# Sliding-window attention and a gated feed-forward block: the first batch loaded by halves of heads, the second transposed 128 wide, and the queues of VectorE and TensorE reordered

## The chip, the cores and the metric

The kernel runs on one core of a Trainium2 chip. The metric is device microseconds of one execution; lower is better. The core has five engines with a queue each, worked off in the order in which the program was recorded: PE (TensorE, matrix products into PSUM), DVE (VectorE), ACT (ScalarE), POOL (GpSimd, which here mostly issues loads) and SP (SyncE, which here issues stores and transposing transfers). "PEld" in the profile is the loading of a product's fixed operand.

## The reference

Eight batches of eight heads, 576 positions, head size 64. A query sees itself and the 127 positions before it, with a penalty that grows linearly with distance and has a slope of its own for each head. The 4608 rows of 512 that result go through a gated feed-forward block with 1536 hidden channels.

```python
B, H, S, D = q.shape                       # 8, 8, 576, 64
scores = np.matmul(q, k.transpose(0, 1, 3, 2)) / np.sqrt(D)
rel = pos[:, None] - pos[None, :]
scores = np.where((rel >= 0) & (rel < 128), scores - slopes * np.abs(rel), -1e9)
attn = softmax(scores)                     # over the keys
x = (attn @ v).transpose(0, 2, 1, 3).reshape(B * S, H * D)
out = (gelu(x @ w_gate) * (x @ w_val)) @ w_out
```

## The kernel before

**Attention.** Inputs are converted to bf16 while they are loaded. The queries and keys of a batch are transposed so that the head size lies on the partitions (`qT`, `kT`); two heads share the 128 partitions, and the four pairs of heads are numbered c = 0 to 3. Positions fall into five blocks of 128 keys, j = 0 to 4, shifted by 64 so that the first half of block 0 is padding. `scores` (L178) makes, for a part s of the queries (part one is queries 0 to 319, part two the rest) and some pairs, the products of keys by queries into PSUM; ACT takes the exponential (L161), and DVE multiplies by a table `emask` that holds penalty and window (L164), in this text "the mask". `scores2` (L166) does the same for block 2 against itself, all pairs in one tile `P2`. `sums` (L203) adds up the probabilities over the keys with products by `ones` and takes the reciprocal on DVE (L218). `spread_pe` (L228) copies the reciprocals to all partitions with products by `sel`, and ACT and DVE bring the result from PSUM into `rb` (L239). `values` (L241) multiplies by v and DVE scales by `rb` into `xT` (L256), the transposed input of the feed-forward block. From batch 4 on the spreading is done by transfers on SP's queue instead.

**Feed-forward.** The 4608 rows are worked in nine groups g of 512. `gate_val` (L262) makes one of 12 hidden channel blocks f of a group: eight products, a gelu on ACT (L273) and a product on DVE (L274). `out_half` (L279) makes half of the sum for 128 output rows, six products; eight such units, numbered 0 to 7, make a group, and after each second one ACT copies the result (L290) and SP stores it. While group g is in work, the attention of a later batch is woven between its units: for g = 0, 1 and 2 the table `todo` writes the order out by hand, from g = 3 on a fixed pattern does it (L399).

**Batches 0 and 1** have to be ready early. Both are loaded in runs (`load_runs`, L101): a partition gets three consecutive positions, or two for the last 192, so that one piece of a transfer holds 192 or 128 numbers; PE transposes them, 64 numbers wide, and the copy out of PSUM puts the positions back into order (`transpose`, `untangle`). Batch 0 does this at the start of the program, batch 1 inside `gate_val` for f = 8 to 11 of group 0, one pair of heads for each f (L412). There both run lengths of a pair go to the same PSUM bank. The batches from 2 on are loaded by blocks of 128 positions (`load`, L81, pieces of 64 numbers) and transposed by transfers on SP's queue.

**What sets the order.** Each engine's queue stands in the order in which the Python code calls it. PSUM has eight banks; `bank()` hands out one that the order has set free, and the product that first writes it waits for the last reader of the tile before. A transfer on POOL's queue waits until the one eight places ahead of it in that queue has landed.

Of the kernel before, what the change touches and what calls it, by code (L numbers as in the profile page):

```python
# [8 lines left out]
BF16 = mybir.dt.bfloat16  # L9
# [17 lines left out]
def kernel(  # L27
# [35 lines left out]
    def bank():  # L63
        return psum.tile([128, 512], FP32, name="ps")
# [23 lines left out]
    def load_qk(b):  # L88
        load(qs[b % 2], q, b)
        load(ks[b % 2], k, b)  # L90
# [4 lines left out]
    def runs(t, n):  # L95
        first, parts, r = RUNS[n]
        lo = 1536 * n
        return t.rearrange("p j x -> p (j x)")[0:parts, lo:lo + 512 * r].rearrange(
            "p (h x) -> p h x", h=H)

    def load_runs(b, n):  # L101
        first, parts, r = RUNS[n]
        for t, src in ((qs[b], q), (ks[b], k)):
            nc.gpsimd.dma_start(
                out=runs(t, n),
                in_=src[b][:, first:first + parts * r, :].rearrange(
                    "h (p r) d -> p h (r d)", r=r))

    def load_v(b):
# [12 lines left out]
    def transpose(b, n, what, c, ps):  # L122

        first, parts, r = RUNS[n]
        src = runs((qs, ks)[what][b], n)
        for x in range(r):
            for i in (0, 1):
                nc.tensor.transpose(  # L128
                    out=ps[64 * i:64 * i + 64, parts * x:parts * x + parts],
                    in_=src[:, 2 * c + i, 64 * x:64 * x + 64],  # L130
                    identity=ident[0:parts, 0:parts])

    def untangle(copy, b, n, what, c, ps):
        first, parts, r = RUNS[n]
        dst = by_pair((qT, kT)[what][b])[:, c, 64 + first:64 + first + parts * r]
        copy(out=dst.rearrange("p (x r) -> p x r", r=r),  # L136
             in_=ps[:, 0:parts * r].rearrange("p (r x) -> p x r", r=r))

    def blocks(t, b, i, c, j, n):
        if b < 2:  # L140
# [34 lines left out]
            exp(P[:, :, i, :], ps[i].rearrange("p (c n) -> p c n", c=4))  # L175
        mask(P.rearrange("p c i n -> p (c i) n"), emask[:, :, 0:128])

    def scores(b, s, cs):  # L178

        pss = []  # L180
        for c in cs:
            ps = [bank(), bank()]
            pss.append(ps)
            for j, qj, n, col in (((0, 0, 2, 0), (1, 1, 2, 256)),
                                  ((4, 4, 1, 0), (2, 3, 1, 128), (3, 3, 2, 256)))[s]:
                for i in (0, 1):
# [110 lines left out]
    for t in qT + kT:  # L297
# [8 lines left out]
    for half, base, step, chan in ((0, 0, 1, -1), (1, -1, -1, 1)):  # L306
# [35 lines left out]
    def rest(cs, copy):  # L342
        for c in cs:
            for w in (0, 1):
                ps = bank().bitcast(BF16)
                transpose(0, 1, w, c, ps)
                untangle(copy, 0, 1, w, c, ps)

    scores(0, 0, (0, 1))
    scores2(0)  # L350
    rest((0, 1), dve)
    scores(0, 0, (2, 3))
    rest((2, 3), dve)
    scores(0, 1, (0, 1))
    sums(0, 0)
    scores(0, 1, (2, 3))
    spread_pe(0, 0)
    values(0, 0, range(4))
# [13 lines left out]
    for t in (qs[0], ks[0]):  # L372
# [4 lines left out]


    todo = {
        0: [("s2", 1), ("s", 1, 0, (0, 1)), 0, ("s", 1, 0, (2, 3)), 1, ("s", 1, 1, (0, 1)),  # L380
            2, ("sum", 1, 0), ("s", 1, 1, (2, 3)), 3, ("spread", 1, 0), ("pv", 1, 0),
            ("sum", 1, 1), 4, 5, ("spread", 1, 1), ("pv", 1, 1), 6, 7],
# [8 lines left out]
    }  # L391

    def steps(g):
# [74 lines left out]
```

## Time and profile before

| | us |
|---|---|
| median of the three timed executions | 381.98 (381.94, 381.98, 469.57) |
| the profiled execution | 379.51 |
| its span, from the first to the last instruction | 377.7 |
| PE busy | 351.2 |
| DVE busy, ACT busy | 191.3, 188.1 |
| POOL busy | 102.5 |

Times in the views are counted from the start of the span of the profiled execution. The profiled execution has 1.8 us around its span, and it was 2.47 us shorter than the median of the timed ones. A row of the timeline gives start, length, engine, line, operation and tiles, the number of instructions, and in brackets the idle time of the engine just before and what ended it. In the chain of waits a row is a stretch of the chain that ended last.

### The profile page before, as it was taken

How to read it: one execution, taken by the hardware profiler on the slowest of the kernel's cores; microseconds unless marked ns; L12 is line 12 of the kernel's file. 1: busy time of each engine (PE TensorE's matmuls, PEld its weight loads, DVE VectorE, ACT ScalarE, POOL GpSimd, SP SyncE). 2: the span in 40 equal slices, each digit the busy share in tenths (PEclk: the TensorE clock that was granted, in tenths of full speed). 3: DMA queues.
4: the chain of work that ended last, by engine and by line, in shares of the span. 5: the costliest groups of instructions: out<-in, count | busy, mean ns of one | idle time of the engine just before them, and what ended most of it. 6: DMA issues, size and time to landing. Idle time of an engine off the chain costs nothing.

```text
span 377.7 us, 6720 instructions
## 1 busy us (share of the span) xinstructions
PE 351.2 (93%) x2696; PEld 171.4 (45%) x2696; DVE 191.3 (51%) x312; ACT 188.1 (50%) x341; POOL 102.5 (27%) x134
## 2 busy tenths in 40 slices
PE   2879869799979998999999999999999999999995
PEld 1545434444444444444544454445444544444442
DVE  2795345833487447756655565556555603312420
ACT  5853339443676537673296339633963223323321
POOL 8934499224305700570290021000000000000000
PEclk9779999999999999999999999999999999999999
DMA  9999999999937992798999599168115020011002
GB/s 111 171 202 194 189 150 132 126 165 174 151 67 75 154 146 41 70 176 122 181 150 144 118 157 113 57 133 135 57 56 128 0 85 28 1 58 56 2 28 84
DMA packets 145408, 41.41 MB, mean 110 GB/s; under 512 B 133056, under 2 KB 138688, under 8 KB 145376
## 3 DMA queue, kind: packets, MB, share of 16 engines
q0 software_dynamic: 106848, 18.88, 63.2%
q1 hardware_dynamic: 38528, 22.10, 26.5%
q8 instruction: 21, 0.34, 0.4%
q14 instruction: 11, 0.09, 0.1%
HBM read 42.47 MB, written 9.51 MB: 138 GB/s over the span
## 4 chain that ended last, share of the span: by engine, by line
PE 84%; ACT 7%; DVE 5%; DMA 2%; issue 1%; POOL 0%; POOLq 0%; ACTq 0%; DVEq 0%
PE ps L269 49%; PE ps L285 22%; ACT P L161 5%; PE ps L250 4%; PE ps L154 3%; PE ps L209 2%; PE ps L232 2%; DMA ks<-in_k_dram 2%; DVE r L218 2%; DVE P L164 2%; PE ps L128 2%; DVE kT L136 1%; ACT L161 1%; ACT qT L136 1%; DVE xT L256 0%
## 5 line engine op out<-in xcount | busy, mean ns | idle before, releaser
L274 DVE TENSOR_TENSOR hT<-ps,gelu 128x512 bf16<-128x512 f32 (+2 forms) x111 | 74.3, 674 | 124.4 <-PE ps L269 113.4
L273 ACT ACTIVATE gelu<-ps 128x512 bf16<-128x512 f32 (+2 forms) x111 | 64.9, 586 | 123.0 <-PE ps L269 122.9
L269 PE MATMUL ps<-xT,wg 128*128 128x512 bf16 (+2 forms) x444 | 112.1, 374 | 0.2
L269 PE MATMUL ps<-xT,wv 128*128 128x512 bf16 (+2 forms) x444 | 111.4, 373 | 0.0
L285 PE MATMUL ps<-wo,hT 128*128 128x512 bf16 x432 | 99.4, 380 | 0.0
L161 ACT ACTIVATE P<-ps 128x512 bf16<-128x512 f32 x144 | 74.2, 635 | 9.5 <-PE ps L154 9.5
L164 DVE TENSOR_TENSOR P<-P,emask 128x1024 bf16<-128x1024 bf16 x72 | 48.9, 686 | 35.3 <-ACT P L161 35.1
L269 PEld LDWEIGHTS <-wv 128*128 128x128 bf16 x444 | 43.3, 98 | 50.3 <-issue 0.2
L269 PEld LDWEIGHTS <-wg 128*128 128x128 bf16 x444 | 41.8, 98 | 48.9 <-issue 0.9
L285 PEld LDWEIGHTS <-hT 128*128 128x128 bf16 x432 | 39.6, 98 | 48.8 <-issue 4.7
L84 POOL DMA_DIRECT2D vb<-in_v_dram x40 | 33.6, 859 | 100.6 <-PE ps L250 73.5
L290 ACT COPY osb<-ps 128x512 f32<-128x512 f32 x36 | 21.9, 610 | 38.7 <-PE ps L285 32.9
L218 DVE RECIPROCAL r<-ps 128x320 f32<-128x320 f32 (+1 forms) x16 | 30.7, 1937 | 0.3 <-PE ps L209 0.3
L84 POOL DMA_DIRECT2D qs<-in_q_dram x30 | 25.3, 889 | 16.2 <-DMA qT<-qs 11.0
L84 POOL DMA_DIRECT2D ks<-in_k_dram x30 | 25.5, 926 | 1.3 <-DMA qs<-in_q_dram 1.3
L256 DVE TENSOR_TENSOR xT<-ps,rb 128x320 bf16<-128x320 f32 (+1 forms) x64 | 24.8, 449 | 0.4 <-DMA rb<-rd 0.4
L154 PE MATMUL ps<-qT,kT 64*128 64x256 bf16 (+1 forms) x384 | 24.0, 253 | 0.9 <-ACT P L161 0.7
L154 PEld LDWEIGHTS <-kT 64*128 64x128 bf16 x384 | 13.6, 97 | 14.2 <-issue 12.5
L250 PE MATMUL ps<-P,vb 128*64 128x128 bf16 (+2 forms) x384 | 18.9, 250 | 0.0
L250 PEld LDWEIGHTS <-vb 128*64 128x64 bf16 x384 | 15.3, 113 | 6.9 <-issue 6.0
L128 PE MATMUL ps<-ident,qs 128*64 128x128 bf16 (+1 forms) x80 | 5.3, 253 | 9.2 <-DMA qs<-in_q_dram 6.8
L209 PE MATMUL ps<-P,ones 128*32 128x128 bf16 (+2 forms) x384 | 11.2, 250 | 2.0 <-DVE P L164 1.6
(41 smaller groups left out, 99.6 us busy)
## 6 DMA issues: line engine op xcount, KB each, us to landing
out_dram<-osb SPq DMA_DIRECT2D x36, 256.0 KB, 2.1
rb<-rd SPq DMA_DIRECT2D x8, 576.0 KB, 7.3
vb<-in_v_dram POOLq DMA_DIRECT2D x32, 128.0 KB, 4.4
qs<-in_q_dram POOLq DMA_DIRECT2D x24, 128.0 KB, 5.7
ks<-in_k_dram POOLq DMA_DIRECT2D x24, 128.0 KB, 5.8
wg<-in_moe_w_gate_dram POOLq DMA_DIRECT2D x4, 384.0 KB, 10.1
wv<-in_moe_w_val_dram POOLq DMA_DIRECT2D x4, 384.0 KB, 11.4
wo<-in_moe_w_out_dram POOLq DMA_DIRECT2D x2, 768.0 KB, 17.1
```

The source lines that it names most:

```text
L84: nc.gpsimd.dma_start(out=t[lo:128, j, :].rearrange("p (h d) -> p h d", h=H), in_=src[b][:, 128 * j - 64 + lo:128 * j + 64, :].rearrange(" ...
L154: nc.tensor.matmul(out=ps[:, col:col + 128 * n].rearrange("p (n t) -> p n t", n=n), lhsT=blocks(kT, b, i, c, j, 1).rearrange("p n t -> p ( ...
L161: nc.scalar.activation(out=dst, in_=src, func=AF.Exp, scale=0.125)
L164: nc.vector.tensor_tensor(out=dst, in0=dst, in1=m, op=ALU.mult)
L218: nc.vector.reciprocal(sumrow[b][:, lo:hi], ps[:, 0:hi - lo])
L250: nc.tensor.matmul(out=ps[64 * i:64 * i + 64, a:e], lhsT=vb[b % 2][:, j, 64 * h:64 * h + 64], rhs=prob(b, s, c, i, j, e - a), start=(j == ...
L256: nc.vector.tensor_tensor(out=xT[:, c, b * S + lo:b * S + hi], in0=ps[:, 0:hi - lo], in1=recip[b][:, c, lo:hi], op=ALU.mult)
L269: nc.tensor.matmul(out=ps[:, 0:hi - lo], lhsT=w[:, c, 128 * f:128 * (f + 1)], rhs=xT[:, c, t0 + lo:t0 + hi], start=(c == 0), stop=(c == 3))
L273: nc.scalar.activation(out=gl[:, 0:hi - lo], in_=pg[:, 0:hi - lo], func=AF.Gelu)
L274: nc.vector.tensor_tensor(out=hid[g][:, f, lo:hi], in0=pv[:, 0:hi - lo], in1=gl[:, 0:hi - lo], op=ALU.mult)
L285: nc.tensor.matmul(out=po, lhsT=hid[g][:, f, 128 * t:128 * (t + 1)], rhs=wo[:, f, :], start=(f == 0), stop=(f == NF - 1))
L290: nc.scalar.copy(out=osb, in_=po)
```

## The change

- Batch 0: the first run length of q and k is loaded in two transfers of four heads each. The first halves of q and k stay at the head of POOL's queue, the second halves stand behind the making of `ident` and of the distances `tmpl`, ahead of the second run length. The transposes of the first two pairs of heads and their part-one scores come before those of the other two. Of the eight copies out of PSUM, ACT now does the two of pair 3 and DVE six; it was four and four.
- Batch 1: loaded by blocks of 128 positions like the later batches, ten transfers in place of four. Each pair of heads is transposed with five 128-wide products for q and five for k, each set into a bank of its own, and one copy for each set brings 640 columns out; it was ten products and two copies for each.
- `scores` gets an argument `then`: the sums of another part, given there, are recorded behind the products of these scores and ahead of their exponentials and masks. It is used for part one's sums at the products of part two, and once for part two's sums of batch 3, at the scores of batch 4. On DVE the reciprocal then stands ahead of those masks.
- `todo` is rewritten for groups 0, 1 and 2 in this sense, with more output units ahead of the spreading and fewer behind it.
- The padding of batch 1 is cleared by DVE at the start and no longer by POOL after group 0; `qT` and `kT` of batch 1 need no clearing any more.

```diff
-    def load_runs(b, n):
+    def load_runs(n, h0, h1):
...
+    def transpose(b, what, c, copy):
+        ps = bank().bitcast(BF16)
+        for j in range(5):
+            nc.tensor.transpose(
+                out=ps[:, 128 * j:128 * j + 128],
+                in_=(qs, ks)[what][b][:, j, 128 * c:128 * c + 128], identity=ident)
+        copy(out=(qT, kT)[what][b][:, :, c, :],
+             in_=ps[:, 0:640].rearrange("p (j t) -> p j t", t=128))
...
-    def scores(b, s, cs):
+    def scores(b, s, cs, then=None):
...
+        if then:
+            sums(*then)
         for c, ps in zip(cs, pss):
...
-    load_runs(0, 0)
+    load_runs(0, 0, 4)
...
-    load_runs(0, 1)
+    load_runs(0, 4, 8)
+    load_runs(1, 0, 8)
...
-    load_runs(1, 0)
-    load_runs(1, 1)
+    for t in (qs[1], ks[1]):
+        nc.vector.memset(t[0:64, 0, :], 0.0)
+    load_qk(1)
...
-    pss = {(w, c): bank().bitcast(BF16) for w in (0, 1) for c in range(4)}
-    for (w, c), ps in pss.items():
-        transpose(0, 0, w, c, ps)
-        untangle((act, dve)[c % 2], 0, 0, w, c, ps)
+    for cs in ((0, 1), (2, 3)):
+        for w in (0, 1):
+            for c in cs:
+                ps = bank().bitcast(BF16)
+                transpose_runs(0, w, c, ps)
+                untangle(act if c == 3 else dve, 0, w, c, ps)
+        if cs[0] == 0:
+            scores(0, 0, cs)
+    scores2(0)
...
-        0: [("s2", 1), ("s", 1, 0, (0, 1)), 0, ("s", 1, 0, (2, 3)), 1, ("s", 1, 1, (0, 1)),
-            2, ("sum", 1, 0), ("s", 1, 1, (2, 3)), 3, ("spread", 1, 0), ("pv", 1, 0),
+        0: [("s2", 1), ("s", 1, 0, (0, 1)), 0, ("s", 1, 0, (2, 3)), 1, 2,
+            ("s", 1, 1, (0, 1), (1, 0)), 3, ("s", 1, 1, (2, 3)), 4, ("spread", 1, 0),
...
                 for w in (0, 1):
-                    ps = bank().bitcast(BF16)
-                    for n in (0, 1):
-                        transpose(1, n, w, f - 8, ps[:, 384 * n:])
-                        untangle((act, dve)[w], 1, n, w, f - 8, ps[:, 384 * n:])
+                    transpose(1, w, f - 8, (act, dve)[w])
...
-        if g == 0:
-            for t in (qs[1], ks[1]):
-                nc.gpsimd.memset(t[0:64, 0, :], 0.0)
```

**DVE at the start of the program.** The first rows behind the clearing of tiles, down to part one's reciprocals of batch 0; the copies with 384 columns bring out the first run length, those with 192 the second, and `TENSOR_TENSOR P` is a mask. Before:

```order
L136 COPY kT_100<-ps 128x384 x2
L164 TENSOR_TENSOR P<-P,emask 128x1024 x2
L164 TENSOR_TENSOR P_253<-P_253,emask 128x1024
L136 COPY qT_98<-ps 128x192
L136 COPY kT_100<-ps 128x192
```

and after:

```order
L136 COPY kT_100<-ps 128x384 x2
L173 TENSOR_TENSOR P<-P,emask 128x1024 x2
L136 COPY qT_98<-ps 128x384
L136 COPY kT_100<-ps 128x384
L173 TENSOR_TENSOR P_261<-P_261,emask 128x1024
L136 COPY qT_98<-ps 128x192
L136 COPY kT_100<-ps 128x192
```

Two copies of 384 columns (pair 2) have come in between the first two masks and the mask of `P2`; they were ACT's.

**POOL, the loads of batch 1** (`qs_95` and `ks_97` are its queries and keys, `vb_103` its values), behind the eight transfers of `wg` and `wv`. Before:

```order
L104 DMA qs_95<-in_q_dram 128x8x192
L104 DMA ks_97<-in_k_dram 128x8x192
L104 DMA qs_95<-in_q_dram 96x8x128
L104 DMA ks_97<-in_k_dram 96x8x128
L368 DMA wo<-in_moe_w_out_dram 128x6x512 x2
L84 DMA vb_103<-in_v_dram 64x8x64
```

and after:

```order
L84 DMA qs_95<-in_q_dram 64x8x64
L84 DMA qs_95<-in_q_dram 128x8x64 x4
L84 DMA ks_97<-in_k_dram 64x8x64
L84 DMA ks_97<-in_k_dram 128x8x64 x4
L384 DMA wo<-in_moe_w_out_dram 128x6x512 x2
L84 DMA vb_103<-in_v_dram 64x8x64
```

Six more transfers, all with pieces of 64 numbers, stand ahead of `wo`.

**DVE behind group 1's `gate_val`**, where the attention of batches 2 and 3 is woven in (`P_1345` and `P_1551`, after the change `P_1303` and `P_1465`, are the `P2` tiles of batches 2 and 3). Before:

```order
L164 TENSOR_TENSOR P_1345<-P_1345,emask 128x1024
L164 TENSOR_TENSOR P<-P,emask 128x1024 x6
L218 RECIPROCAL r<-ps 128x320
L164 TENSOR_TENSOR P<-P,emask 128x1024 x2
L239 COPY rb<-ps 128x320 x2
L256 TENSOR_TENSOR xT<-ps,rb 128x320 x4
L164 TENSOR_TENSOR P_1551<-P_1551,emask 128x1024
L218 RECIPROCAL r<-ps 128x256
```

and after:

```order
L173 TENSOR_TENSOR P_1303<-P_1303,emask 128x1024
L173 TENSOR_TENSOR P<-P,emask 128x1024 x4
L230 RECIPROCAL r<-ps 128x320
L173 TENSOR_TENSOR P<-P,emask 128x1024 x4
L173 TENSOR_TENSOR P_1465<-P_1465,emask 128x1024
L251 COPY rb<-ps 128x320 x2
L268 TENSOR_TENSOR xT<-ps,rb 128x320 x4
L173 TENSOR_TENSOR P<-P,emask 128x1024 x2
```

The reciprocal has gone ahead of two masks; the mask of batch 3's `P2` has gone ahead of the copies into `rb`, and two masks of batch 3 stand ahead of the second reciprocal, which follows the rows shown.

More of the change, by code (lines that the diff above doesn't have):

```diff
@@ L99, in runs @@
             "p (h x) -> p h x", h=H)
-    def load_runs(b, n):
+    def load_runs(n, h0, h1):
         first, parts, r = RUNS[n]
-        for t, src in ((qs[b], q), (ks[b], k)):
+        for t, src in ((qs[0], q), (ks[0], k)):
             nc.gpsimd.dma_start(
-                out=runs(t, n),
-                in_=src[b][:, first:first + parts * r, :].rearrange(
+                out=runs(t, n)[:, h0:h1, :],
+                in_=src[0][h0:h1, first:first + parts * r, :].rearrange(
                     "h (p r) d -> p h (r d)", r=r))
@@ L120, in by_pair, with transpose_runs @@
         return t.rearrange("p j c t -> p (j c t)").rearrange("p (c x) -> p c x", c=4)
-    def transpose(b, n, what, c, ps):
+    def transpose_runs(n, what, c, ps):
         first, parts, r = RUNS[n]
-        src = runs((qs, ks)[what][b], n)
+        src = runs((qs, ks)[what][0], n)
         for x in range(r):
@@ L131, in transpose, with untangle @@
                     identity=ident[0:parts, 0:parts])
-    def untangle(copy, b, n, what, c, ps):
+    def untangle(copy, n, what, c, ps):
         first, parts, r = RUNS[n]
-        dst = by_pair((qT, kT)[what][b])[:, c, 64 + first:64 + first + parts * r]
+        dst = by_pair((qT, kT)[what][0])[:, c, 64 + first:64 + first + parts * r]
         copy(out=dst.rearrange("p (x r) -> p x r", r=r),
              in_=ps[:, 0:parts * r].rearrange("p (r x) -> p x r", r=r))
+    def transpose(b, what, c, copy):
[6 more added lines that the diff above has]
+             in_=ps[:, 0:640].rearrange("p (j t) -> p j t", t=128))
     def blocks(t, b, i, c, j, n):
-        if b < 2:
+        if b == 0:
             return by_pair(t[b])[64 * i:64 * i + 64, c, 128 * j:128 * (j + n)].rearrange(
@@ L292, in out_half @@
             nc.sync.dma_start(out=out[r0:r0 + 128, :], in_=osb)
-    load_runs(0, 0)
+    load_runs(0, 0, 4)
     nc.vector.memset(ident, 0.0)
-    for t in qT + kT:
+    for t in (qT[0], kT[0]):
         nc.vector.memset(by_pair(t)[:, :, 0:64], 0.0)
@@ L336, with rest @@
     act, dve = nc.scalar.copy, nc.vector.tensor_copy
-    pss = {(w, c): bank().bitcast(BF16) for w in (0, 1) for c in range(4)}
-    for (w, c), ps in pss.items():
-        transpose(0, 0, w, c, ps)
-        untangle((act, dve)[c % 2], 0, 0, w, c, ps)
-    def rest(cs, copy):
+    for cs in ((0, 1), (2, 3)):
[7 more added lines that the diff above has]
+    scores2(0)
+    def rest(cs):
         for c in cs:
@@ L345, in rest @@
                 ps = bank().bitcast(BF16)
[L346 to L351, printed above, removed]
+                transpose_runs(1, w, c, ps)
+                untangle(dve, 1, w, c, ps)
+    rest((0, 1))
     scores(0, 0, (2, 3))
-    rest((2, 3), dve)
-    scores(0, 1, (0, 1))
-    sums(0, 0)
+    rest((2, 3))
+    scores(0, 1, (0, 1), (0, 0))
     scores(0, 1, (2, 3))
@@ L379 @@
     todo = {
-        0: [("s2", 1), ("s", 1, 0, (0, 1)), 0, ("s", 1, 0, (2, 3)), 1, ("s", 1, 1, (0, 1)),
-            2, ("sum", 1, 0), ("s", 1, 1, (2, 3)), 3, ("spread", 1, 0), ("pv", 1, 0),
-            ("sum", 1, 1), 4, 5, ("spread", 1, 1), ("pv", 1, 1), 6, 7],
[8 rows of a table removed]
[11 rows of a table added]
     }
```

17 rows, old and new, of the table todo are left out of this document.

## The prediction

> **What bounds the kernel now.** I read the page first, then the chain of waits in order of time, then the timeline around each place where the chain leaves PE.
>
> ```profile
> PE 351.2 (93%) x2696; PEld 171.4 (45%) x2696; DVE 191.3 (51%) x312; ACT 188.1 (50%) x341; POOL 102.5 (27%) x134
> ...
> PEclk9779999999999999999999999999999999999999
> DMA  9999999999937992798999599168115020011002
> ```
>
> PE works for 93% of the span, so the change can only win what lies in the other 26.5 us (377.7 less 351.2), and what is busy but stretched. That time lies ahead of group 3; behind it the program is unchanged. The transfers are busy throughout the first quarter, which matters for a change that adds transfers there. Three kinds of place are touched: batch 1's transposes, the hand-written orders behind groups 0 to 2, and the start.
>
> The chain of waits at f = 9 of group 0:
>
> ```profile
> 47.77 0.31 PE ps L128 x6
> 48.10 0.49 ACT qT L136
> ...
> 48.63 0.46 PE ps L128 x10
> ...
> 49.11 0.57 DVE kT L136
> ...
> 49.72 0.28 PE ps L128 x4
> 50.00 1.83 PE ps L269 x8
> ```
>
> Here the chain walks from PE to ACT, back, to DVE, and back. The four products of the second run length wait until the copy of the first has left their bank, for q and again for k: from 47.77 to 50.00, 2.23 us, of which 1.05 are products. Nothing else covers the two waits, because PE's queue holds these products ahead of the next `gate_val`.
>
> **Term 1, batch 1's transposes, f = 8 to 10.** The timeline has the first products of f = 8 and f = 11, and the 24 transposes of batch 0's keys:
>
> ```profile
> 8.84 1.49 PE L128 MATMUL ps<-ident,ks 128*64 128x128 bf16 x24 [0.53 <-DMA ks<-in_k_dram]
> ...
> 43.64 0.36 PE L128 MATMUL ps<-ident,qs 128*64 128x128 bf16 x6
> ...
> 55.85 0.36 PE L128 MATMUL ps<-ident,qs 128*64 128x128 bf16 x6
> ```
>
> Three rounds take 12.21 us, 4.07 each, 1.83 of them `gate_val`. After the change a round is `gate_val` and ten transposes with no wait between, since each set of five has a bank of its own. A 128-wide transpose is not in the trace. The 64-wide ones come every 62 ns (1.49 by 24), which gives 0.62 a round. I take 0.62, the nearest row, and 1.73 for `gate_val` once it is not preceded by a wait (an estimate: 1.83 less the 0.1 that its first product lags); a round is 2.35, and three win 3 × 1.72 = **5.1**. If PE needed twice the time for twice the width, 1.24, the term is 3.3; below 0.62 there is little to win.
>
> The copies must not become the bound. Their groups:
>
> ```profile
> L164 DVE TENSOR_TENSOR P<-P,emask 128x1024 bf16<-128x1024 bf16 x72 | 48.9, 686 | 35.3 <-ACT P L161 35.1
> ...
> L136 DVE COPY kT<-ps 128x384 bf16<-128x384 bf16 x6 | 3.3, 558 | 3.1 <-PE ps L128 3.0
> ...
> L136 ACT COPY qT<-ps 128x384 bf16<-128x384 bf16 x6 | 2.9, 479 | 2.8 <-PE ps L128 2.8
> ```
>
> ```profile
> L274 DVE TENSOR_TENSOR hT<-ps,gelu 128x512 bf16<-128x512 f32 (+2 forms) x111 | 74.3, 674 | 124.4 <-PE ps L269 113.4
> L273 ACT ACTIVATE gelu<-ps 128x512 bf16<-128x512 f32 (+2 forms) x111 | 64.9, 586 | 123.0 <-PE ps L269 122.9
> ```
>
> In proportion to the columns, 640 take at most 0.93 on DVE and 0.80 on ACT. With the 0.67 and 0.59 of `gate_val`, both engines stay at or under 1.6 of a round of 2.35, so the copies hide.
>
> **The transfers that this needs.** The keys of batch 1 are now the last of ten transfers with 9216 pieces (eight times 1024 and two times 512) in place of 3584. POOL's waits tell when things landed: the transfer of 32.78 waited for the last `wv`, that of 34.83 for the first q load of batch 1, 1024 pieces.
>
> ```profile
> 24.27 0.77 POOL L104 DMA_DIRECT2D ks<-in_k_dram  x1 [1.26 <-DMA wv<-in_moe_w_val_dram]
> ...
> 32.78 0.88 POOL L84 DMA_DIRECT2D vb<-in_v_dram  x1 [0.72 <-DMA wv<-in_moe_w_val_dram]
> 34.83 0.87 POOL L84 DMA_DIRECT2D vb<-in_v_dram  x1 [1.18 <-DMA qs<-in_q_dram]
> ```
>
> ```profile
> ks<-in_k_dram POOLq DMA_DIRECT2D x1, 192.0 KB, 14.5
> ```
>
> The last k load landed at 24.27 + 14.5 = 38.8, so the four took 6.0 us behind the weights. For small pieces, the stretch from 46 to 60 us, all of 64 numbers:
>
> ```profile
> DMA packets 16234, 2.08 MB, mean 148 GB/s; under 512 B 16230, under 2 KB 16231, under 8 KB 16231
> ```
>
> 16234 pieces in 14 us are 0.86 ns each; 9216 take 7.9 us, and the last key lands at about 40.7. PE asks for it at 43.6, so there are 3 us in hand: cost **0**. `wo` lands 2 us later than before, the values of batch 1 as well; they are wanted more than 5 us later than they landed, and POOL's issues (under 0.9 us each) keep ahead of the landings. The clearing moved to DVE's start and POOL's two after group 0 cost nothing.
>
> **Term 2, the woven orders.** The rows that set them:
>
> ```profile
> 58.72 5.00 ACT L161 ACTIVATE P<-ps 128x512 bf16<-128x512 f32 x10
> ...
> 66.82 2.15 DVE L218 RECIPROCAL r<-ps 128x320 f32<-128x320 f32 x1
> ...
> 72.42 1.75 DVE L218 RECIPROCAL r<-ps 128x256 f32<-128x256 f32 x1
> ...
> 106.31 0.66 PE L209 MATMUL ps<-P,ones 128*32 128x192 bf16 x21 [0.74 <-DVE P L164]
> ...
> 115.19 1.76 DVE L218 RECIPROCAL r<-ps 128x256 f32<-128x256 f32 x1 [0.16 <-PE ps L209]
> ...
> 121.91 1.03 PE L269 MATMUL ps<-xT,wg 128*128 128x512 bf16 x4
> ...
> 143.27 0.68 PE L209 MATMUL ps<-P,ones 128*32 128x192 bf16 x24
> ...
> 146.59 2.15 DVE L218 RECIPROCAL r<-ps 128x320 f32<-128x320 f32 x1
> ...
> 153.15 1.76 DVE L218 RECIPROCAL r<-ps 128x256 f32<-128x256 f32 x1 [0.17 <-PE ps L209]
> ...
> 163.76 1.04 PE L269 MATMUL ps<-xT,wg 128*128 128x512 bf16 x4
> ```
>
> An output unit, from the chain of waits, and the copy behind each second one, from the groups:
>
> ```profile
> 118.73 1.40 PE ps L285 x6
> ```
>
> ```profile
> L290 ACT COPY osb<-ps 128x512 f32<-128x512 f32 x36 | 21.9, 610 | 38.7 <-PE ps L285 32.9
> ```
>
> *Group 0.* With one q copy of at most 0.80 in place of two with a wait between, ACT starts its table load and then the ten exponentials earlier against the round's start, by an estimated 0.3. They, not PE, pace the stage: from 58.45 the ten take 5.0, the last part-one mask 0.7, so it ends at 64.2 and the sums at 64.8, and the reciprocal starts at 64.9 in place of 66.82. What is late next is DVE itself: four masks are now queued behind it. 64.9 + 2.1 + 4 × 0.65 + 0.9 (copies to `rb`) + 1.7 (`xT`) puts the second reciprocal at 72.2, only 0.2 before the old 72.42. Behind it one output unit is left in place of two, worth 1.4. Together **+1.6**.
>
> *Group 1.* The sums end at 106.9 as before; two units are done by then instead of one. But the reciprocal's end does not release the copies to `rb`: ahead of them on both ACT and DVE now stand batch 3's `P2` exponentials and mask. ACT: the third unit ends at 108.3 and its copy at 108.9, then six exponentials of 0.5 until 112.0; DVE: the mask until 112.7, `rb` to 113.6, `xT` to 115.3, then two masks that wait for their exponentials until 117.1. The second reciprocal starts at 117.1 in place of 115.19; one unit fewer follows. 1.9 later against 1.4: **-0.5**.
>
> *Group 2.* The reciprocal starts when the sums end, 143.95 in place of 146.59, and the second one at about 152.0 (2.1, four masks 2.6, 0.9, 1.7, the mask of `P2` 0.7) in place of 153.15. The same work follows both: **+1.1**.
>
> Each of these carries perhaps 0.7 either way.
>
> **Term 3, the start.**
>
> ```profile
> 6.82 1.49 PE L128 MATMUL ps<-ident,qs 128*64 128x128 bf16 x24 [6.82 <-DMA qs<-in_q_dram]
> ...
> 9.74 1.20 DVE L136 COPY kT<-ps 128x384 bf16<-128x384 bf16 x2 [0.82 <-PE ps L128]
> ...
> 22.90 0.89 DVE L239 COPY rb<-ps 128x320 f32<-128x320 f32 x2 [0.48 <-PE ps L232]
> ...
> 23.70 1.75 DVE L256 TENSOR_TENSOR xT<-ps,rb 128x320 bf16<-128x320 f32 x4
> ```
>
> q and k landed at 6.8 and 8.8, so halves of them land near 5.8, 6.8, 7.8 and 8.8, and DVE's first k copies end at 9.0 in place of 10.94. But DVE then has two masks that wait for four exponentials (until about 11.6), two copies more than before (1.2), and the mask of `P2`, whose scores wait for those copies and whose exponentials take another 1.0. It reaches that mask near 14.4, against 14.0 before. From there its queue is full: masks, eight copies, the reciprocal, four masks. The copies to `rb` come at 22.9 to 23.4. I take **-0.3**. The bounds are -1.0 (another wait of that kind) and +1.9 (the whole head start survives).
>
> **Sum.** 5.1 + 1.6 - 0.5 + 1.1 - 0.3 = 7.0 us. The profiled execution, 379.51, becomes 372.5; it lay 2.47 under the median of the timed ones, so the time is 381.98 - 7.0 = **375.0**.
>
> **Rivals.**
>
> *The start pays.* If the halves land earlier than in proportion, DVE's idle time is not refilled and the 1.9 us survive: 375.0 - 2.2 = 372.8. For it: `xT` at 23.70 hangs on DVE alone. Against it: the queue above. 0.18.
>
> *The woven orders give nothing.* `rb` and the reciprocals queue behind masks in all three groups as I found for group 1: group 0 +0.3, group 1 -1.2, group 2 0. Then 375.0 + 3.1 = 378.1. 0.14.
>
> *128-wide transposes do not overlap.* The trace's transposes use half the width each and may run in pairs. If a wide one kept PE for the whole length of a row here, a round would hold 10 × 0.266:
>
> ```profile
> L128 PE MATMUL ps<-ident,ks 128*64 128x128 bf16 x48 | 2.9, 266 | 0.5 <-DMA ks<-in_k_dram 0.5
> ```
>
> That is 2.66 and a round of 4.4; term 1 turns to -1.0, and the time is 375.0 + 6.1 = 381.1. Against it: 24 of that length fit in 1.49 us. 0.05. [...]
>
> *The small pieces come too late, and it is slower.* Over the whole span the software queue's packets cost more than in the stretch above:
>
> ```profile
> q0 software_dynamic: 106848, 18.88, 63.2%
> ```
>
> 63.2% of 16 engines for 377.7 us, by 106848, is 35.7 ns of one engine; 9216 packets on 16 engines then take 20.6 us and the last key lands at 53.4. PE would stand at its transposes from 43.6 on, 9.8 us, which eats the 7.0: 384.8. The change is a loss as soon as that key lands behind 50.6. Against it: the 0.86 ns measured on just such pieces. 0.05. [...]
>
> **How the numbers follow.** The forecast has 0.58; its own range is 373.2 to 376.8, from the 0.7 of each woven stage and the bounds of terms 1 and 3. A measurement of this kernel can tell about 2% from no change, 7.6 us: the line is at 374.3. Of the forecast's 0.58 some 0.2 lies below it, with the first rival 0.38 faster. Slower by over 2% would need 389.6, which only the last rival reaches if `wo` and the values come late as well: 0.02. The rest, 0.60, is within 2%. The range from 371.2 to 378.8 takes in the forecast, the first rival and most of the second.
>
> **What would show it.** Rounds of f = 8 to 10 of about 2.35 with no idle PE between the transposes and no wait of theirs on a transfer; `rb` of batch 0 at about 23; the second reciprocals of batches 1, 2 and 3 earlier by 0.2, later by 1.9 and earlier by 1.1 against the start of their stage, and the first product of groups 1, 2 and 3 following. PE waiting for `ks` near 44, a round over 3 us, or `rb` at 21 would make the prediction wrong.

## The result and the profile after

The changed kernel takes 370.55 us (median of four executions, 370.51 to 370.83) against 381.96 of before (four executions): a ratio of 0.971, 95% interval 0.969 to 0.973; the ratio leaves out the one slow execution of before, 469.57 us. That is 11.4 us less, where 7.0 were forecast, and 0.65 us below the range; it is faster by 2.9%, and for more than 2% the prediction gave 0.38. The profiled execution of after took 370.55 us as well, span 368.8; that of before took 379.51, span 377.7. So the two traces differ by 8.9 us and the timed executions by 11.4. Both gaps have to be explained.

The page of after, busy times of the engines and the granted clock over the span:

```profile
PE 351.2 (95%) x2656; PEld 171.4 (46%) x2656; DVE 190.3 (52%) x310; ACT 186.9 (51%) x335; POOL 107.9 (29%) x140
...
PEclk9999999999999999999999999999999999999999
```

PE is busy for 351.2 us as before. So the 8.9 us between the traces are time in which PE had stood still. The view of PE's waits from 43 to 80 us (waited for: us in total, times, longest) shows the larger part of it. Before:

```profile
PE ps L128 <- DVE kT L136: 2.6, 4, 0.6
PE ps L128 <- ACT qT L136: 2.3, 4, 0.6
PE ps L232 <- DVE r L218: 2.0, 1, 2.0
```

After:

```profile
PE ps L244 <- DVE r L230: 0.5, 1, 0.5
PE ps L163 <- DVE kT L145: 0.4, 1, 0.4
PE ps L221 <- DVE P L173: 0.3, 1, 0.3
PE ps L163 <- ACT P L170: 0.2, 1, 0.2
```

The eight waits between the two run lengths are gone, and the wait for the first reciprocal of batch 1. PE's timeline of after, from f = 8 to the first products of groups 1, 2 and 3 (L142 are the new transposes, L281 `gate_val`, L244 the spreading):

```profile
43.08 0.44 PE L142 MATMUL ps<-ident,qs 128*128 128x128 bf16 x5
43.36 0.44 PE L142 MATMUL ps<-ident,ks 128*128 128x128 bf16 x5
43.63 1.03 PE L281 MATMUL ps<-xT,wg 128*128 128x512 bf16 x4
...
49.93 0.44 PE L142 MATMUL ps<-ident,qs 128*128 128x128 bf16 x5
...
67.89 0.71 PE L244 MATMUL ps<-r,sel 32*128 32x256 f32 x8 [0.46 <-DVE r L230]
...
70.84 1.03 PE L281 MATMUL ps<-xT,wg 128*128 128x512 bf16 x4
...
114.51 1.03 PE L281 MATMUL ps<-xT,wg 128*128 128x512 bf16 x4
...
155.24 1.04 PE L281 MATMUL ps<-xT,wg 128*128 128x512 bf16 x4
```

Set against the starts of before (43.64, 55.85, 78.56, 121.91, 163.76), stage by stage:

| stage | before, us | after, us | won | forecast |
|---|---|---|---|---|
| up to the transposes of f = 8 | 43.64 | 43.08 | 0.56 | -0.3 |
| rounds f = 8 to 10 | 12.21 | 6.85 | 5.36 | 5.1 |
| f = 11's transposes to group 1 | 22.71 | 20.91 | 1.80 | 1.6 |
| group 1 | 43.35 | 43.67 | -0.32 | -0.5 |
| group 2 | 41.85 | 40.73 | 1.12 | 1.1 |
| behind it, with the last store | 213.9 | 213.6 | 0.4 | 0 |
| span | 377.7 | 368.8 | 8.9 | 7.0 |

The 0.4 us of the last stage lie behind the last copy of a result, in the last store (3.6 us from the copy's end to the end of the span, then 3.2). No run shows why it is shorter.

### The profile page after: what moved, and what is told of

It reads as the page before. It is cut to its first block, busy times and chain, and to the rows that moved or that the text cites. A ratio compares the mean times of both kernels' runs of the same rounds, so it can differ in the third digit from the quotient of the medians.

```text
span 368.8 us, 6643 instructions
## 1 busy us (share of the span) xinstructions
PE 351.2 (95%) x2656; PEld 171.4 (46%) x2656; DVE 190.3 (52%) x310; ACT 186.9 (51%) x335; POOL 107.9 (29%) x140
## 3 DMA queue, kind: packets, MB, share of 16 engines
HBM read 42.47 MB, written 9.51 MB: 141 GB/s over the span
## 4 chain that ended last, share of the span: by engine, by line
PE 85%; ACT 7%; DVE 5%; DMA 1%; issue 1%; POOL 0%; POOLq 0%; DVEq 0%; ACTq 0%
PE ps L281 50%; PE ps L297 23%; ACT P L170 6%; PE ps L163 4%; PE ps L262 4%; PE ps L221 2%; DVE r L230 2%; DVE P L173 2%; DMA ks<-in_k_dram 1%; PE ps L244 1%; DVE xT L268 1%; ACT L170 1%; PE ps L128 1%; PE ps L142 1%; ACT osb L302 0%
## 5 line engine op out<-in xcount | busy, mean ns | idle before, releaser
L281 PE MATMUL ps<-xT,wg 128*128 128x512 bf16 (+2 forms) x444 | 112.2, 374 | 0.3
L281 PE MATMUL ps<-xT,wv 128*128 128x512 bf16 (+2 forms) x444 | 111.4, 373 | 0.0
L281 PEld LDWEIGHTS <-wv 128*128 128x128 bf16 x444 | 43.3, 98 | 50.5 <-issue 0.5
L281 PEld LDWEIGHTS <-wg 128*128 128x128 bf16 x444 | 41.9, 98 | 48.7 <-issue 0.9
L84 POOL DMA_DIRECT2D qs<-in_q_dram x35 | 29.6, 885 | 25.0 <-DMA qT<-qs 13.2
L84 POOL DMA_DIRECT2D ks<-in_k_dram x35 | 29.8, 898 | 6.7 <-DMA qs<-in_q_dram 3.8
L221 PEld LDWEIGHTS <-ones 128*32 128x32 bf16 x384 | 8.2, 99 | 5.7 <-issue 5.3
```

What stands on the lines that cost most here:

```text
L84: nc.gpsimd.dma_start(out=t[lo:128, j, :].rearrange("p (h d) -> p h d", h=H), in_=src[b][:, 128 * j - 64 + lo:128 * j + 64, :].rearrange(" ...
L221: nc.tensor.matmul(out=ps[32 * c:32 * c + 32, a:e], lhsT=ones[:, min(j, 1), i, :], rhs=prob(b, s, c, i, j, e - a), start=(i == 0 and j == ...
L281: nc.tensor.matmul(out=ps[:, 0:hi - lo], lhsT=w[:, c, 128 * f:128 * (f + 1)], rhs=xT[:, c, t0 + lo:t0 + hi], start=(c == 0), stop=(c == 3))
```

## Experiments

**One part of the change at a time.** Three kernels each put one part into the kernel before, and one is the kernel before itself, timed more often with its clocks.

Before, unchanged:

> The kernel before, unchanged. Theory: what the prediction missed is the TensorE clock. The profiled execution of before had half the clock from 14.3 to 24.5 us (mean 0.984) and took 379.51 us, 2.4 us less than the 381.96 of the timed ones, while the changed kernel shows 1.000 and one and the same time, 370.5 to 370.8, in all its executions. Then these executions spread from 379.5 to 382 and the mean clock falls as the time grows, to about 0.97 at 382. Rival: the clock is 0.984 in all of them whatever the time, and the 2.4 us lie elsewhere, in a transfer for one.

Its twelve executions took 379.5 to 382.4 us, median 381.55; 23 executions of before beside them 379.2 to 382.4, median 381.56. They come in clusters, not evenly: of the 23, four lie at 379.2 to 379.6 and nineteen at 381.0 to 382.4, none between. The recorded mean clock does not fall with the time: 0.984 goes with 379.2 and with 381.1, 0.993 with 382.0. It says little either way, because the record leaves out half rate at the start (see the last section). This kernel's profiled execution was one of the longer ones (span 380.3). PE's timeline in group 0, and the window 71 to 74 us (busy time of PE, PEld, DVE, ACT and POOL, then the mean granted clock, DMA share and GB/s):

```profile
70.19 0.82 PE L232 MATMUL ps<-r,sel 32*128 32x320 f32 x8 [2.01 <-DVE r L218]
70.94 1.82 PE L250 MATMUL ps<-P,vb 128*64 128x192 bf16 x24
72.69 1.04 PE L209 MATMUL ps<-P,ones 128*32 128x128 bf16 x24
73.67 3.27 PE L285 MATMUL ps<-wo,hT 128*128 128x512 bf16 x12
```

```profile
71.00:74.00 3.00, 3.00 (x51) 2.15 (x50) 2.79 (x8) 0.75 (x2) 0.92 (x2) 0.55 0.08 31
```

Behind the 2.01 us in which PE stands waiting for the reciprocal, the clock falls to half, and the values, the second sums and the two units take 1.82, 1.04 and 3.27 us. The profiled execution of before has the same standing, and the same work takes 1.18, 0.62 and 2.76:

```profile
69.12 0.82 PE L232 MATMUL ps<-r,sel 32*128 32x320 f32 x8 [2.01 <-DVE r L218]
69.87 1.18 PE L250 MATMUL ps<-P,vb 128*64 128x192 bf16 x24
70.98 0.62 PE L209 MATMUL ps<-P,ones 128*32 128x128 bf16 x24
71.54 2.76 PE L285 MATMUL ps<-wo,hT 128*128 128x512 bf16 x12
74.31 0.71 PE L232 MATMUL ps<-r,sel 32*128 32x256 f32 x8
```

The lengths overlap, so the loss is read from the starts: from one spreading to the next it is 5.19 us here and 6.68 there (70.19 to 76.87), 1.49 us more. The other 1.07 us by which this execution is longer were lost by the start (f = 8 at 44.71 and not 43.64): the second sums and the first `gate_val` products of batch 0 ran slowly (1.04 for the 24 sums, 0.62 in the first profile).

The start alone:

```diff
-    load_runs(0, 0)
+    load_runs(0, 0, 0, 4)
...
-    load_runs(0, 1)
+    load_runs(0, 0, 4, 8)
+    load_runs(0, 1)
...
-    scores(0, 1, (0, 1))
-    sums(0, 0)
+    scores(0, 1, (0, 1), (0, 0))
```

> Before, with the new start of batch 0 alone (loads and transposes by halves of heads, six copies on DVE, reciprocal of part one ahead of part two's masks); batch 1 and the woven orders of groups 0 to 2 as before. The traces give 0.46 us at the first product of group 0's long stretch. Theory (the clock, and the start is what keeps it up): clock 1.000, 0.5 + 2.4 = 2.9 us, 379.1. If the clock loss hangs on something else: clock as in before, 381.5. The prediction's -0.3 us would be 382.3.

380.18 us, ratio 0.996 (0.994 to 0.998): 1.4 us less than before. Its f = 8 comes at 43.16 in place of 43.64 in the first profile and of 44.71 in the one above. The clock theory fails here: the start does not keep the clock up. Its profiled execution had the standing of 2.01 us in group 0 and half rate behind it (2.13 us for the 24 values), and its executions spread from 378.1 to 381.5 as those of before do.

Batch 1's transposes alone:

```diff
-    load_runs(1, 0)
-    load_runs(1, 1)
+    load_qk(1)
...
-                    for n in (0, 1):
-                        transpose(1, n, w, f - 8, ps[:, 384 * n:])
-                        untangle((act, dve)[w], 1, n, w, f - 8, ps[:, 384 * n:])
+                    transpose128(1, w, f - 8, (act, dve)[w])
```

> Before, with batch 1 loaded by blocks of 128 positions and transposed 128 wide, one bank and one copy for each set; start and woven orders as before. The prediction's term 1 says 5.1 us, the traces 5.4 to 5.8 (one q copy more at the head of group 0's exponentials): 376.3 to 376.9, the clock still below 1.000 since the start is the old one. Rival (this edit is what restores the clock): 2.4 us more, about 374.

373.75 us, ratio 0.981 (0.979 to 0.984): 7.8 us less. By its trace three rounds take 6.86 us (5.35 won) and the stage of group 0 22.32 in place of 22.71 (0.39 won). That is 5.7 us. The other 2 fit the clock, so the rival was right on the time: the standing of 2.01 us is still there, but in this trace the values behind it take 1.18 us. Five of six executions lie within 373.3 to 374.2, the sixth at 375.88.

The woven orders alone (`then` and `todo` for groups 0 to 2):

```diff
-            2, ("sum", 1, 0), ("s", 1, 1, (2, 3)), 3, ("spread", 1, 0), ("pv", 1, 0),
-            ("sum", 1, 1), 4, 5, ("spread", 1, 1), ("pv", 1, 1), 6, 7],
+            ("s", 1, 1, (0, 1), (1, 0)), 3, ("s", 1, 1, (2, 3)), 4, ("spread", 1, 0),
+            ("pv", 1, 0), 5, ("sum", 1, 1), 6, ("spread", 1, 1), ("pv", 1, 1), 7],
```

> Before, with the new orders of groups 0, 1 and 2 alone (sums recorded ahead of part two's exponentials and masks, more output units ahead of the spreading); start and batch 1's transposes as before. The prediction's terms sum to 2.2 us, the traces to 2.6 (1.8 - 0.3 + 1.1), of which 0.4 in group 0 belong to the single q copy: 379.4 to 379.8. Rival (the orders give nothing by themselves and group 0 gained only through the transposes): 381.2, since groups 1 and 2 alone leave 0.8.

378.17 us, ratio 0.992 (0.990 to 0.994): 3.4 us less. Its trace gives 1.41, -0.31 and 1.11 us for the three groups. PE's timeline in group 0:

```profile
69.25 0.82 PE L234 MATMUL ps<-r,sel 32*128 32x320 f32 x8
...
75.00 0.71 PE L234 MATMUL ps<-r,sel 32*128 32x256 f32 x8 [0.46 <-DVE r L220]
...
77.96 1.03 PE L271 MATMUL ps<-xT,wg 128*128 128x512 bf16 x4
```

The spreading waits for nothing any more. With the 0.39 from the run before, group 0's 1.80 is complete. (That 0.39 hangs on the waits among f = 11's transposes and not on the number of copies: split banks, below, keep two copies and win 0.46 there.) The three parts together would be 12.6 us; the whole change gave 11.0 beside the same 381.6. The difference, 1.6, is about one loss of 1.49: the transposes and the orders each avoid it, and it can be avoided once.

**What makes the clock fall in group 0.**

```diff
+    def fill(n):
+        ps = bank()
+        for _ in range(n):
+            nc.tensor.matmul(out=ps, lhsT=warm[:, 0:128], rhs=warm, start=True, stop=True)
...
-            2, ("sum", 1, 0), ("s", 1, 1, (2, 3)), 3, ("spread", 1, 0), ("pv", 1, 0),
+            2, ("sum", 1, 0), ("s", 1, 1, (2, 3)), 3, ("fill", 8), ("spread", 1, 0), ("pv", 1, 0),
```

> Before, with eight products that compute nothing (128 by 512, into a bank that nobody reads, 1.7 us) between unit 3 and the spreading of group 0, where PE stands for 2.01 us. Nothing else is changed. Theory (the standing makes the clock fall): the executions above 381.1 disappear, those at 379.2 to 381.1 stay; median about 380.5, values of that stage 1.18 us and not 1.82. Rival (the clock falls for another reason, or the loss is only at the start): as before, 381.5, some executions at 382.

380.29 us, and all twelve executions between 379.5 and 380.7; of the 17 of before beside them fourteen are longer than that. PE's timeline (L341 is the filler):

```profile
67.47 1.89 PE L341 MATMUL ps<-warm 128*128 128x512 bf16 x8
69.65 0.82 PE L233 MATMUL ps<-r,sel 32*128 32x320 f32 x8 [0.28 <-DVE r L219]
70.40 1.18 PE L251 MATMUL ps<-P,vb 128*64 128x192 bf16 x24
```

With work that computes nothing in the gap, the values take 1.18 us. The standing is the cause of the loss in group 0. What is left, 1.2 us from the shortest to the longest, fits the start: f = 8 comes at 43.64 to 45.00 us in the traces with the old start.

```diff
             gate_val(g, f)
+            if g == 0 and f == 5:
+                fill(8)
             if g == 0 and f >= 8:
```

> Before, with eight products that compute nothing (1.73 us at full rate) behind the sixth channel block of group 0, in a stretch without waits: everything behind is 1.73 us later, the standing of 2.01 us in group 0 too, and nothing else changes. [...] Rival (any standing of 2 us is caught in the same share): 383.3, four in five above 382.5.

383.3 would be the 381.6 of before with the 1.73 added, if the clock fell in nineteen of 23 executions as there. It took 382.20 us beside a median of 381.03: 1.73 us of added work cost 1.2. Less 1.73, nine of the twelve executions lie at 379.4 to 380.6, within 0.15 us of the range of the filled kernel, and three at 380.9 to 381.0; of the 16 of before beside them eleven lie at 380.9 or above. So behind the same standing of 2.01 us, moved by 1.73 us, the clock falls, by the times, in at most a quarter of the executions and no longer in most.

Does the changed kernel do without?

> The changed kernel, unchanged. Theory: of the executions of before the slow ones (381.8 to 382.4) lose about 1.6 us in group 0, where PE stands still for 2 us ahead of the spreading and then runs the values, the second sums and two units at half rate; the changed kernel has 0.46 us of standing there, so its times do not spread: all within 370.3 to 371.0. Rival: its four executions were lucky, and some of twelve are 1 to 3 us longer, as those of before are.

370.65 us, four executions from 370.2 to 371.2, a little wider than the first four. None of the eight carries, by its time, a loss of 1.5 us on top; a spread of 1.0, as in the filled kernel, remains.

**Wait or width?** Before, with a bank for each run length, 64 wide as before:

```diff
-                    ps = bank().bitcast(BF16)
                     for n in (0, 1):
-                        transpose(1, n, w, f - 8, ps[:, 384 * n:])
-                        untangle((act, dve)[w], 1, n, w, f - 8, ps[:, 384 * n:])
+                        ps = bank().bitcast(BF16)
+                        transpose(1, n, w, f - 8, ps)
+                        untangle((act, dve)[w], 1, n, w, f - 8, ps)
```

> Before, with the two run lengths of batch 1's pairs in a bank each: still loaded in runs, still 64-wide products and two copies for each set, but the second length no longer waits for the copy of the first. It takes the wait of term 1 away without the width. Theory: twelve products at about 56 ns and eight at about 42 ns make 1.0 beside 1.73 of the group's products, a round of 2.75 in place of 4.07 (2.28 in after), so 4.0 us of the 5.4 come from the wait and 1.4 from the width; with up to 2 us of clock as in the run with the transposes alone: 375.6 to 377.6. Rival (the copies, four in a round, pace it): rounds over 3.0, 378 or more.

374.65 us, ratio 0.984 (0.981 to 0.986): 6.4 us less. PE's timeline:

```profile
45.00 0.45 PE L128 MATMUL ps<-ident,qs 128*64 128x128 bf16 x10
45.28 0.42 PE L128 MATMUL ps<-ident,ks 128*64 128x128 bf16 x10
45.63 1.04 PE L269 MATMUL ps<-xT,wg 128*128 128x512 bf16 x4
...
47.46 0.44 PE L128 MATMUL ps<-ident,qs 128*64 128x128 bf16 x10
```

A round is 2.46 us, better than the 2.75 expected: the twenty narrow products start within 0.63 us, ten of them within the 0.28 that five wide ones take. In the program they go in turn to different halves of the bank's partitions; why two come in the time of one wide product, no run shows. Of the 5.36 us in the rounds 4.8 come from the separate banks, and only 0.5 from the width and the new loads.

**Group 1's loss.**

```diff
-            ("s", 2, 1, (0, 1), (2, 0)), 3, ("s", 2, 1, (2, 3)), ("s2", 3), ("spread", 2, 0),
-            ("pv", 2, 0), 4, ("s", 3, 0, (0, 1)), 5, ("sum", 2, 1), 6, ("spread", 2, 1),
+            ("s", 2, 1, (0, 1), (2, 0)), 3, ("s", 2, 1, (2, 3)), 4, ("spread", 2, 0),
+            ("pv", 2, 0), 5, ("sum", 2, 1), ("s2", 3), ("s", 3, 0, (0, 1)), 6, ("spread", 2, 1),
             ("pv", 2, 1), ("s", 3, 0, (2, 3)), 7],
```

> The changed kernel, with batch 3's P2 scores and the first scores of its part one put behind the second sums of batch 2 in group 1's order, and one more unit ahead of the first spreading. The prediction's reading of group 1 (-0.5, the trace says -0.32): the mask and exponentials of batch 3's P2 stand ahead of the copies to rb, and the masks of batch 3 ahead of the second reciprocal. If that is the cause, the reciprocal starts at about 106.5 in place of 109.18 and the group is 1.0 to 2.0 us shorter: 368.5 to 369.5. Rival (ACT's exponentials pace the group, the order behind them matters little): 370.3 to 370.6.

369.35 us, ratio to before 0.969 (0.967 to 0.972). The timeline of DVE and PE:

```profile
106.39 1.76 DVE L230 RECIPROCAL r<-ps 128x256 f32<-128x256 f32 x1
...
108.43 0.71 PE L244 MATMUL ps<-r,sel 32*128 32x256 f32 x8
...
113.13 1.03 PE L281 MATMUL ps<-xT,wg 128*128 128x512 bf16 x4
```

The reciprocal starts 35.6 us after group 1's first product (at 70.76) in place of 38.3, PE no longer waits for it, and the group takes 42.37 us in place of 43.67. So the cause was the one that the prediction read off group 1's queues.

**Variants beyond.** All three orders changed; in group 0 the second sums between spreading and values, in group 2 directly behind the values:

```diff
-            ("pv", 1, 0), 5, ("sum", 1, 1), 6, ("spread", 1, 1), ("pv", 1, 1), 7],
+            ("sum", 1, 1), ("pv", 1, 0), 5, 6, ("spread", 1, 1), ("pv", 1, 1), 7],
...
-            ("pv", 3, 0), ("s2", 4), 2, ("s", 4, 0, (0, 1), (3, 1)), 3, ("spread", 3, 1),
+            ("pv", 3, 0), ("sum", 3, 1), ("s2", 4), 2, ("s", 4, 0, (0, 1)), 3, ("spread", 3, 1),
```

> The changed kernel with all three woven orders changed: group 1 as in the run before (1.38 us by its trace), in group 0 the second sums moved between the spreading and the values (0.46 us of waiting), in group 2 the second sums directly behind the values (0.47 us). Theory: the waits for the second reciprocals go, 2.3 us in all, 368.2. Rival (what is late next takes it back: in group 0 the values' banks are held longer by DVE): 369.3.

369.06 us (368.5 to 369.5), ratio 0.969 (0.967 to 0.972). Groups 1 and 2 take 42.36 and 40.20 us (1.3 and 0.5 less); group 0's stage takes 20.99, 0.1 more than in after, because PE now waits 0.5 us for a mask ahead of the second sums, as the rival said of that group. With 1.5 us less than the changed kernel this is the fastest of the study, level with the group 1 variant within what can be told.

Warm-up products at the start:

```diff
+    fill(8)
     act, dve = nc.scalar.copy, nc.vector.tensor_copy
...
     scores(0, 1, (2, 3))
+    fill(4)
     spread_pe(0, 0)
```

> The changed kernel, with products that compute nothing: eight 128 by 512 ahead of the first transposes, while PE waits for the first q, and four in its wait for the first reciprocal. In the trace of after, PE's products up to 25.2 us take about twice what the same shapes take later (scores 64 by 128, twelve: 1.03 against 0.61; values of 24: 2.13 against 1.18), though the granted clock is told as 1.00. Theory: PE starts at half rate and only a filled stretch brings full rate; then the 5.6 us of PE on the chain up to there shrink by 1.0 to 2.4: 368.2 to 369.5, scores of twelve 0.61. Rival (DVE and ACT pace the start, PE is hidden): 370.0 to 370.6; if the eight products delay the first transposes: up to 371.3.

370.24 us (370.1 to 370.9), no difference to the changed kernel that can be told. PE's timeline:

```profile
1.54 3.59 PE L355 MATMUL ps<-warm 128*128 128x512 bf16 x8 [1.54 <-DVE warm L310]
5.07 0.56 PE L129 MATMUL ps<-ident,qs 128*64 128x128 bf16 x12
...
22.48 1.18 PE L263 MATMUL ps<-P,vb 128*64 128x192 bf16 x24
...
24.46 1.39 PE L282 MATMUL ps<-xT,wg 128*128 128x320 bf16 x4 [0.24 <-DVE xT L269]
```

The products are fast behind the filler (0.56 for twelve transposes that took 0.85, 1.18 for the values that took 2.13), but `gate_val` then waits for DVE. So it does in after_again, where the values took 1.18 without a filler, so a filler is not the only way to full rate. The rival held: DVE paces the start. With the filler of three in the wait for the first reciprocal alone, on top of the new orders of groups 1 and 2:

> The changed kernel with the new orders of groups 1 and 2 of the run before (1.31 and 0.53 us by its trace; group 0 as in the change, since its new order gave nothing), and three products that compute nothing in the wait for batch 0's first reciprocal, where PE stands 1.4 us and afterwards runs values and sums at half rate in some executions. Theory: 370.6 - 1.8 = 368.8, and the filled wait keeps the first block of group 0 from starting up to 0.7 us later: 367.9 to 368.8, executions within 0.5 us. Rival (the filler delays the spreading more than it saves): 369.0 to 369.5.

369.1 us (five executions at 368.7 to 369.2, one at 372.4). PE's first `gate_val` again waits for `xT`, 0.69 us, and the second half of k landed late (10.16 against 9.51): the filler brings nothing. The one long execution shows that an order without the standing is not safe from every loss; where it lost was not traced.

## Why the prediction was right and wrong

The predicted time was 4.45 us too high. 1.9 of it lie in the terms: 0.86 in term 3, 0.40 in term 2, 0.26 in term 1 (0.06 of it rounding, as 3 × 1.72 is 5.16), and 0.4 in the last store, which was put at nothing. The other 2.5 lie in the last step of "Sum".

**The step that failed** is "it lay 2.47 under the median of the timed ones, so the time is 381.98 - 7.0". It carried the 2.47 over to the changed kernel as if it lay around the span. It lay inside it: by their times, most executions of before lose 1.49 us in group 0, where PE runs at half rate because it had stood for 2.01 us ahead of the spreading, and up to 1.2 us at the start. The profiled execution was one of the few without the first loss, and its start was a quick one. The change takes that wait away (2.01 to none), and with it the loss. The shortest executions show the change without this: 379.2 of before against 370.2 of after is 9.0, as the traces. Without the step the forecast would have been the 372.5 that "Sum" has one line earlier, and what the traces won, taken from 379.51, gives 370.6. The prediction quoted the wait's row nowhere and asked of no row what clock stands behind a wait.

**Term 1** was right in kind and 0.26 short. The transposes need 0.56 us a round, not 0.62. That 0.62 came so near was luck: the row of 62 ns stands at the start of the program, where products run at half rate (twelve transposes take 0.85 us there in after and 0.56 in the run with warm-up products). Where the change works, narrow transposes come every 28 ns (ten within 0.28 us with split banks), and a wide one, at 56, does cost twice that. The copies hide: 0.69 on ACT and 0.48 on DVE for 640 columns, below the 0.80 and 0.93 of the bounds. What the term did not separate is that the bank, not the width, is worth nine tenths of it. The rival on 128-wide transposes falls by the same rows: five start within 0.28 us, though each lasts 0.22.

**The transfers** held as argued: PE's rows at 43.08 and 43.36 have no wait on `qs` or `ks`, so the rival on the small pieces falls.

**Term 2.** DVE's second reciprocals in after, of batches 1, 2 and 3:

```profile
66.08 1.76 DVE L230 RECIPROCAL r<-ps 128x256 f32<-128x256 f32 x1
...
109.18 1.75 DVE L230 RECIPROCAL r<-ps 128x256 f32<-128x256 f32 x1
...
144.64 1.76 DVE L230 RECIPROCAL r<-ps 128x256 f32<-128x256 f32 x1 [0.43 <-PE ps L221]
```

Against the first product of its stage the first starts 0.4 us earlier than before (16.15 for 16.57; forecast 0.2), the second 1.7 later (38.34 for 36.63; forecast 1.9). Batch 3's starts 1.1 earlier (30.13 for 31.24), as forecast. The groups gave 1.80, -0.32 and 1.12 for 1.6, -0.5 and 1.1: three queues followed instruction by instruction came within 0.2 us each. The rival that the orders give nothing falls.

**Term 3** has the wrong sign. The start in after, PE and DVE:

```profile
4.91 0.85 PE L128 MATMUL ps<-ident,qs 128*64 128x128 bf16 x12 [4.91 <-DMA qs<-in_q_dram]
6.49 0.85 PE L128 MATMUL ps<-ident,ks 128*64 128x128 bf16 x12 [0.73 <-DMA ks<-in_k_dram]
```

```profile
13.64 0.69 DVE L173 TENSOR_TENSOR P<-P,emask 128x1024 bf16<-128x1024 bf16 x1 [1.60 <-ACT P L170]
...
18.30 2.16 DVE L230 RECIPROCAL r<-ps 128x320 f32<-128x320 f32 x1 [0.40 <-PE ps L221]
...
22.72 0.88 DVE L251 COPY rb<-ps 128x320 f32<-128x320 f32 x2
```

The halves landed at 4.9 and 6.5 us, not at 5.8 and 6.8. `P2`'s mask comes at 13.64, not 14.4, the reciprocal at 18.30 (0.8 earlier than before), and `rb` at 22.72, 0.2 earlier than before. The mechanism, a full DVE queue behind `P2`'s mask that eats the head start, was right: of 1.9 us some 0.2 are left at `rb`. At f = 8 it is 0.56, of which a part is the clock, since full rate came at 24.02 us and not at 24.54. What was mis-sized most plainly is the landing of the first halves; no run varies it. The rival "The start pays", at 372.8, came nearest to the time, but not for its reason.

## What to carry to other kernels

Before a profiled time is scaled to timed ones, ask what the difference is: if the executions fall into clusters, look for waits of PE with slow products behind them, since an edit that removes such a wait can win back what those products lose too (here 1.49 us behind a wait of 2.01). Look for pairs of tiles that share a PSUM bank with nothing between them: here the copy's round trip cost 1.6 us of a round of 4.07 with two such pairs, and a bank each won 4.8 of the 5.36 us that the change won in its three rounds, without another layout. And a reciprocal moved forward in a queue is worth only what does not stand between it and its readers (in group 1 the new order, with the reciprocal ahead of two masks, cost 0.32 us); that can be read off the order, one instruction after another.

## What the runs showed of the hardware

- **A wait of 2.01 us was followed by half TensorE's clock in some executions, and its place in time counted.** By their times the clock fell behind a standing of 2.01 us in nineteen of 23 executions, in none of twelve with the gap filled, and in at most three of twelve with the gap moved by 1.73 us. In the trace of before_again the window of 71 to 74 us, shown above, has a mean clock of 0.55. The next one (columns as there, the clock third from the end):

```profile
74.00:75.00 1.00, 1.00 (x4) 0.40 (x3) 1.00 (x1) 0.00 (x0) 0.65 (x1) 0.64 0.75 48
```

  If a window's mean is split between full and half, the half rate goes from 71.30 to 74.72, which is 3.42 us. The half-rate stretch in the first profile of before begins and ends within these windows:

```profile
14.00:14.50 0.50, 0.38 (x5) 0.23 (x4) 0.50 (x1) 0.50 (x2) 0.50 (x1) 0.80 1.30 140
14.50:24.00 9.50, 6.79 (x88) 4.67 (x89) 9.02 (x19) 6.67 (x14) 5.63 (x8) 0.50 1.29 197
...
24.30:24.60 0.30, 0.30 (x10) 0.28 (x6) 0.30 (x2) 0.30 (x1) 0.30 (x1) 0.59 1.34 207
```

  It goes from 14.3 to 24.55, 10.25 us or three times as long.

  Six traces have this standing of 2.01 us. In two of them the 24 values behind it are slow, 1.82 us (before_again) and 2.13 (the start alone), and the windows put the fall of the clock 1.1 and about 0.4 us behind the end of the standing: 71.30 for 70.19, and some 69.04 for 68.64, from a mean of 0.88 between 66 and 70 us. In the four others (before, split banks, the moved gap, the transposes alone) the values take 1.18. (By their times all six executions with split banks and five of six with the transposes alone show no loss.) What sets the two apart from the four is not shown.
- **The record of the clock begins with its first change.** In after the 24 values products take 2.13 us; the view's clock from 22 to 26 us is 1.00 (columns as above):

```profile
21.99 2.13 PE L262 MATMUL ps<-P,vb 128*64 128x192 bf16 x24
```

```profile
22.00:26.00 4.00, 3.94 (x61) 2.97 (x58) 4.00 (x9) 2.45 (x4) 1.75 (x2) 1.00 1.31 203
```

  In a second execution of the same kernel, after_again, the same products take 1.18:

```profile
21.29 1.18 PE L262 MATMUL ps<-P,vb 128*64 128x192 bf16 x24
```

  The trace of after has no record of the clock ahead of 24.02 us, where it becomes full and where the slow values end. The view counts what lies ahead of the first record as 1.00. So neither a 1.00 there nor an execution's mean clock says that PE ran at full rate; the lengths of known products do. The spread of the start fits this: in before, the filled kernel, before_again and split banks, all with the old start, the first four `gate_val` products of batch 0 take 0.72, 0.82, 1.24 and 1.25 us, the next four 0.71, 0.71, 0.74 and 1.11, and f = 8 comes at 43.64, 44.17, 44.71 and 45.00.
- **Transposes.** Five 128-wide ones start within 0.28 us, 56 ns each (after); of the 64-wide ones, which go in turn to different halves of a bank's partitions, ten do (split banks), 28 ns each. The copy of 640 columns that lie in order took DVE 0.48 us (after), while one of 384 that it puts into order took 0.55 (after) to 0.56 (before).
